# The last pass of a decode backward kernel: a different order of the stages, and buffers kept apart for stores

## The chip, the cores and the metric

The kernel runs on one core of a Trainium2 chip, as one launch. The metric is device time in microseconds. A core has five engines with queues of their own: TensorE (PE, matmuls; PEld is its weight load), VectorE (DVE), ScalarE (ACT), GpSimd (POOL) and SyncE (SP). In this kernel SyncE issues every load from HBM and GpSimd issues every store; the transfers of both run on the core's 16 DMA engines.

## The reference, cut to what matters

One token runs through two layers, twice: attention over a long cache (A), then a two-layer network with a squared ReLU (B), then A and B again with the same weights. The reference gives the output and the gradients of all inputs, the caches among them. The pass that the change touches computes the gradients of the caches and of the queries.

```python
# B, Sq, D = 1, 1, 1024;  Hq, Hkv, Sk, Dh = 32, 4, 65536, 128;  F = 3584
def _A_ref(x, k_cache, v_cache, wq, wo):
    q = (x @ wq).reshape(B, Sq, Hq, Dh).transpose(0, 2, 1, 3)
    k = jnp.repeat(k_cache, rep, axis=1)
    v = jnp.repeat(v_cache, rep, axis=1)
    p = _softmax(jnp.einsum("bhqd,bhkd->bhqk", q, k) * (Dh ** -0.5))
    o = jnp.einsum("bhqk,bhkd->bhqd", p, v)
    return o.transpose(0, 2, 1, 3).reshape(B, Sq, Hq * Dh) @ wo

def _fwd_reference(...):
    x = A_x
    x = x + _A_ref(_layernorm(x), A_k_cache, A_v_cache, A_wq, A_wo)
    x = x + _B_ref(_layernorm(x), B_w1, B_b1, B_w2, B_b2)
    x = x + _A_ref(_layernorm(x), A_k_cache, A_v_cache, A_wq, A_wo)
    x = x + _B_ref(_layernorm(x), B_w1, B_b1, B_w2, B_b2)
    return x
# the result: the output, and jax.vjp of it for grad_out
```

K and V hold 4 groups of 65536 rows of 128 values in bf16, 64 MiB each. Their gradients (out_2 for K, out_3 for V) have the same size. For each cache row and both layers, dP = V dO, dS = P (dP - delta), dV = sum of P dO, dK = sum of dS q, dQ = sum of dS K.

## The kernel before, in words

**Passes.** The kernel reads the caches four times. Passes 1 and 2 are the forward attention of the two layers, pass 3 (`attn_bwd3`) the backward of the second layer's queries, and pass 4 (`attn_bwd4`), the last, does the rest: dQ of the first layer, and dK and dV of both layers together. Between the passes lie dense stages for B and the weights. The change touches pass 4 alone.

**Blocks and items.** A block is 1 MiB of K or V: 32 chunks of 128 rows (`J = 32`). There are 64 blocks of each, 16 per group. Pass 4 goes over 256 items of 8 chunks, four to a block, in a reversed order of groups. For each item, `pipeline` calls a list of stages, each at its own lag in steps:

- `vT` transposes V on TensorE (L1319), and an evacuation (a copy out of PSUM, through `evac`, L161 on ScalarE or L164 on VectorE) writes `kt`. Seven V blocks come out of pass 3 transposed already and skip this.
- `vS` multiplies by dO (L1350) into `ps_sc`; at the end of a block VectorE multiplies by P (L1367) and has dS, called X.
- `eIn` and `eT` copy P of the block on GpSimd (L1328) and transpose it (L1334). P of both layers lies in eight buffers of the arena ("planes", two per group), which are given back when their group is done.
- `dV8` and `dK8` make dV and dK by rank-16 products (`outer16`, L1390): two 512-wide matmuls fill one of two PSUM buffers `ps_gg`, an evacuation writes 1024 columns into a buffer of the arena, and after four of these GpSimd issues a store of 1 MiB (L1396).
- `xT` transposes X for dK; `k8` multiplies K by X into `ps_acc` for dQ (L1421).

**Background work.** `Background.step` is called once per step. It advances the gradients of the weights (`g_outer`, store at L1507; `g_outer_wide`, store at L1528) and the rows of wo and wq that the next group needs (`g_rowdots`: VectorE product at L583, ScalarE sum at L572). The gradient slabs are evacuated through `ps_gg` too (L1467), four evacuations to a 1 MiB store.

**Who sets the order.** Passes 1 to 3 stand in a manual schedule; pass 4 doesn't: a scheduler of the framework orders the instructions of each engine, from the order in which the program emits them and the data they need. Each engine then runs its instructions strictly in that order. So a wait at the head of an engine's queue holds all that is behind it.

**The arena.** Twenty buffers of 1 MiB, of which eight hold P at first. Each load and each store needs one. `take_one` chooses it when the program is built, from a table FREE of when each buffer comes free, counted in steps; a stored buffer counts as free five steps later. Before the change, in pass 4, a load takes the latest freed buffer that has been free for `AHEAD = 9` steps, or else the oldest; an output takes the latest that has been free for one step. Loads and outputs thus take over one another's buffers. A load into a buffer that a store has left waits, on SyncE, until that store has landed.

**Lags before.** `V_SHIFT` lets the V stages lead the others by 16 items (four blocks) at first; the lead falls to nothing over the first 64 items. `eIn` runs 16 steps after its item's number, dV and dK follow at lags 3 and 7 behind it, and `k8` comes last, at lag 11. Two K blocks are loaded before the pass; some loads are issued by hand (`nexts`, with `NOW["newest"]`), and the last three V blocks by `last_v` in one go. dS of the first eight blocks has a buffer of the arena (Xs) until the first group is done; later blocks use three buffers of a pool.

**End.** When dQ of the last group is there, `on4` runs the rows of wq (L667, L699), the layer norm's backward, dx, and the last slab of wq's gradient (`g_outer_last`, L1467, four stores of 512 KiB, L1488).

Of the kernel before, what the change touches and what calls it, by code (L numbers as in the profile page):

```python
# [10 lines left out]
BF = mybir.dt.bfloat16  # L11
# [9 lines left out]
def kernel(  # L21
# [50 lines left out]
    AHEAD = 9  # L72
# [189 lines left out]
    HELD, BUSY = set(), set()  # L262
    NOW = {"step": 0, "pairs": True, "wide": False, "newest": False}
# [19 lines left out]
    def take_one(fill, load=False):  # L283
        by_age = sorted((t, i) for i, t in FREE.items())
        if load and NOW["newest"]:
            i = by_age[-1][1]
            del FREE[i]
            return i
        if load and PS["pass4"]:
            early = [i for t, i in by_age if t <= NOW["step"] - AHEAD]  # L290
            i = early[-1] if early else by_age[0][1]
            del FREE[i]
            return i
        if fill:
# [86 lines left out]
    def touch_order(items, stages):  # L381
        seen, out = set(), []
        at = sorted((k + (lag(k) if callable(lag) else lag), n, k) for n, (t, lag) in enumerate(stages) for k in range(len(items)))
# [13 lines left out]
    B4_LAG = DK_LAG + J // 8  # L397
    DV_LAG = TLEAD + 1
    V_LEAD = 4 * J // 8
    ITEMS = [order_by_unit(False, SU), order_by_unit(True, SU), order_by_unit(False, HB), order_by_unit(True, J)]  # L400
    V_SHIFT = lambda k: min(V_LEAD, max(0, (k - V_LEAD) // 3))
    TOUCH = [touch_order(ITEMS[0], [("k", 0), ("v", FWD_LAG)]), touch_order(ITEMS[1], [("k", 0), ("v", FWD_LAG)]),
             touch_order(ITEMS[2], [("v", 0), ("k", B3_LAG)]), touch_order(ITEMS[3], [("v", V_SHIFT), ("k", B4_LAG + V_LEAD)])]
# [193 lines left out]
    class Rows:  # L597
        def __init__(self, pool=None, bufs=NWT):
            self.pool, self.bufs = pool, bufs
            self.views = deque()  # L600
            self.n = 0
            self.parts = 0
            if pool is None:

                for _ in range(2):
                    t = Slot("s_wt", True).t[:, :].rearrange("p (v a b) -> p v a b", v=4, a=8)
                    self.views.extend(t[:, v, :, :] for v in range(4))
                self.bufs = 8
            self.queue = deque()
            self.jobs = deque()  # L610
            self.feed = None
# [150 lines left out]
    class Background:  # L762
# [35 lines left out]
        def by_group(self, p, gen):  # L798

            order = list(dict.fromkeys(g for g, _ in ITEMS[p]))  # L800
            n = len(ITEMS[p]) // G
            for k, g in enumerate(order[1:]):
                self.later.append((k * n + 8 if PS["pass4"] and k else k * n + n // 4, gen(g), g))
# [21 lines left out]
    def pipeline(items, stages, bg, end=(), holds=(), lead=None):  # L825

        def due(lag):
            at = {}
            for k, it in enumerate(items):
                at.setdefault(k + lag + LEAD if lead is None or lag >= 0 else k + ~lag + lead(k), []).append(it)  # L830
            return at
        LEAD = 0 if lead is None else lead(len(items))
        when = [due(l) for _, l in stages]
        maxlag = max(l for _, l in stages) + LEAD
        for i in range(len(items) + maxlag):
# [11 lines left out]
            bg.step(max(0, i - LEAD))  # L847
# [415 lines left out]
    def attn_bwd4(p, La, Lb, on_group, bg, stack, end=()):  # L1263
# [75 lines left out]
        def vS(g, c8):  # L1339
# [12 lines left out]
            if is_turned("v", g, c8):  # L1352
                kv_done("v", g, c8)
                if c8 % J == J - 8 and nexts:
                    NOW["newest"] = True
                    kv8(*nexts.popleft())
                    NOW["newest"] = False
            if (c8 + 8) % J == 0:
                c0 = c8 + 8 - J
                ps_dp = state["ps_dp"]  # L1360
                if g == items[0][0]:
                    if c8 == J - 8 + items[0][1]:
                        state["Xs"] = Slot("xs", True)
                    X = state["Xs"].t.rearrange("p (n j r) -> p n j r", j=J, r=R2)[:, c0 // J % 8, :, :]
                else:
                    X = dspool.tile([P, J, R2], BF, name="X", tag="X", bufs=3)
# [42 lines left out]
        def k8(g, c8):  # L1409
# [15 lines left out]
            if (g, c8) == items[len(items) // G - 1]:  # L1425
                state["Xs"].free()
# [6 lines left out]
        for b in range(2):  # L1433
            kv8("k", *items[b * J // 8])
        nexts = deque()
        for b in range(V_LEAD * 8 // J // 2):
            nexts.append(("k",) + items[(b + 2) * J // 8])
            nexts.append(("v",) + items[(b + NKEEP[2]) * J // 8])
        pipeline(items, [(vT, ~0), (vS, ~TLEAD), (eIn, 0), (eT, TLEAD), (dV8, DV_LAG), (xT, DK_LAG - 1), (dK8, DK_LAG), (k8, B4_LAG)], bg,
                 end, lead=V_SHIFT)  # L1440

# [28 lines left out]
    def g_outer_last(pool, out_dram, a_cols, b_cols, c0):  # L1470
# [6 lines left out]
        sls = [Slot("og", True) for _ in ras]  # L1477
# [33 lines left out]
    def g_outer_wide(pool, out_dram, nA, nB, a_cols, b_cols):  # L1511

        rsl = Slot("rowbw", True)
# [242 lines left out]
    def last_v():  # L1756

        for g, c8 in ITEMS[3][-3 * J // 8::J // 8]:
            kv8("v", g, c8)

# [8 lines left out]
    attn_bwd4(3, L1, L3, on4, bg, b4, [(12 + B4_LAG, last_v), (20, pre_load("wq4", lambda: wq_slabs(lastg[3], 2))), (10, fill4)])  # L1769
# [32 lines left out]
```

## Time and profile before

| what | value |
|---|---|
| runs of the kernel, median (lowest to highest) | 2014.15 us (2004.31 to 2018.07), 3 runs |
| span of the profiled execution | 2011.2 us; what lies around it isn't listed, the nearest time is the runs' median |
| busy share of the span | PE 81%, PEld 66%, DVE 58%, ACT 52%, POOL 7% |
| DMA over the span | 794.98 MB, mean 395 GB/s; HBM read 624.96 MB, written 165.69 MB |
| pass 4 | about 1215 us to the end |
| loads of pass 4, issue to landing, median | K 11.6 us (61 x 1 MiB), V 11.0 us (57 x 1 MiB) |
| stores of pass 4, issue to landing | 10.4 us median, 21.4 us longest (149 x 1 MiB) |

How to read it: the page's second part cuts the span into 40 slices, with each engine's busy tenths, the clock that TensorE was granted (PEclk) and the DMA's share and rate. A table by stretch gives the same for chosen times: busy us of each engine with its instruction count, then the mean granted clock, the DMA share and GB/s. A row of waits names the waiting engine and line, what it waited for, us in total, times, and the longest. A row of the timeline gives start and duration, engine, line, what is done, and in brackets the idle time before it and what ended it. Times in MB and GB/s are decimal; a buffer of 1 MiB is 1.05 MB.

### The profile page before, as it was taken

Reading aid. Unit: us, or ns where it says so; the run is one execution under the profiler, and the core shown is the slowest. Engines: PE = TensorE matmul, PEld = TensorE weight load, DVE = VectorE, ACT = ScalarE, POOL = GpSimd, SP = SyncE. Lnnn points to the kernel's source line nnn. Section 1 sums busy time; section 2 is a strip of 40 time slices with the busy share of each in tenths; the row PEclk is TensorE's granted clock in tenths of the full one; section 3 lists DMA queues with packets and bytes.
Section 4 is the critical chain, followed back from the end, with each engine's and each line's share of the span. In section 5 each row is a group of like instructions: output and inputs, shape, how many; then the busy total and the mean of one; then the engine's idle time right before and its main releaser. Section 6 shows DMA issues by size and latency. Waiting matters only on the chain. (4 is left out here: it accounts for less than half of the span.)

```text
span 2011.2 us, 67084 instructions
## 1 busy us (share of the span) xinstructions
PE 1627.2 (81%) x30228; PEld 1319.5 (66%) x30228; DVE 1171.7 (58%) x2426; ACT 1045.1 (52%) x1608; POOL 142.9 (7%) x332
## 2 busy tenths in 40 slices
PE   6877788687877777878787888788789799977887
PEld 6877777687777776767777785455455465644554
DVE  5645555255545544435454477656677677866775
ACT  3534344253433453426354365656678576756765
POOL 0000000000000000000000001111111111111211
PEclk9989999699999998899888999878898877888996
DMA  9999999999999998899999987998999999999996
GB/s 390 421 424 420 424 424 402 395 405 420 425 420 424 425 391 335 356 421 424 417 420 412 394 311 284 360 377 350 394 418 424 423 411 370 418 423 388 424 404 243
DMA packets 101037, 794.98 MB, mean 395 GB/s; under 512 B 9472, under 2 KB 9486, under 8 KB 37134
## 3 DMA queue, kind: packets, MB, share of 16 engines
q1 hardware_dynamic: 76670, 624.99, 76.2%
q0 software_dynamic: 24080, 165.70, 20.0%
q8 instruction: 236, 3.87, 0.8%
q14 instruction: 51, 0.42, 0.1%
HBM read 624.96 MB, written 165.69 MB: 393 GB/s over the span
## 5 line engine op out<-in xcount | busy, mean ns | idle before, releaser
L164 DVE COPY kt<-ps_tr 128x1024 bf16<-128x1024 bf16 x724 | 496.4, 688 | 489.8 <-PE ps_tr L1007 252.6
L161 ACT CAST arena<-ps_gg 128x1024 bf16<-128x1024 f32 x457 | 446.9, 1012 | 234.2 <-PE ps_gg L1390 161.6
L1007 PE MATMUL ps_tr<-ident_b,arena 128*128 128x128 bf16 x3840 | 306.9, 224 | 45.6 <-DMA arena<-in_A_k_cache_dram 33.3
L161 ACT COPY kt<-ps_tr 128x1024 bf16<-128x1024 bf16 x164 | 170.9, 1047 | 191.7 <-PE ps_tr L1199 113.5
L1007 PEld LDWEIGHTS <-arena 128*128 128x128 bf16 x3840 | 231.4, 100 | 54.1 <-DMA arena<-in_A_k_cache_dram 36.5
L1109 PE MATMUL ps_acc<-arena 128*128 128x64 bf16 (+4 forms) x4096 | 203.8, 195 | 67.5 <-DMA arena<-in_A_v_cache_dram 53.8
L164 DVE CAST arena<-ps_gg 128x1024 bf16<-128x1024 f32 (+2 forms) x186 | 222.2, 1195 | 61.5 <-PE ps_gg L1390 32.4
L1390 PE MATMUL ps_gg<-GG,xt 64*128 64x512 bf16 x1024 | 221.5, 433 | 21.5 <-ACT arena L161 13.1
L1319 PE MATMUL ps_tr<-ident_b,arena 128*128 128x128 bf16 x1824 | 186.6, 240 | 39.1 <-DMA arena<-in_A_v_cache_dram 37.7
L1109 PEld LDWEIGHTS <-arena 128*128 128x128 bf16 x4096 | 157.7, 100 | 73.2 <-DMA arena<-in_A_v_cache_dram 57.4
L1090 ACT ACTIVATE arena<-S_sb,L_negm 128x128 bf16<-128x128 f32 x256 | 165.5, 1003 | 62.4 <-DVE L_negm L1075 62.4
L1199 PE MATMUL ps_tr<-ident_b,arena 128*128 128x128 bf16 x1920 | 157.9, 229 | 43.8 <-DMA arena<-in_A_v_cache_dram 41.6
L1025 PE MATMUL ps_sc<-L_qpad,kt 128*128 128x64 bf16 (+7 forms) x3584 | 181.7, 193 | 14.2 <-ACT kt L161 6.6
L1319 PEld LDWEIGHTS <-arena 128*128 128x128 bf16 x1824 | 123.9, 107 | 98.0 <-issue 56.1
L1025 PEld LDWEIGHTS <-kt 128*128 128x128 bf16 x3584 | 151.2, 100 | 19.3 <-ACT kt L161 8.9
L1199 PEld LDWEIGHTS <-arena 128*128 128x128 bf16 x1920 | 119.8, 103 | 49.3 <-DMA arena<-in_A_v_cache_dram 44.7
L1421 PEld LDWEIGHTS <-arena 128*128 128x128 bf16 x2048 | 97.8, 105 | 73.4 <-issue 47.5
L1090 ACT ACTIVATION_READ_ACCUMULATOR arena<-S_sb,L_negm 128x1 f32 x256 | 128.1, 500 | 0.0
L1350 PEld LDWEIGHTS <-kt 128*128 128x128 bf16 x1824 | 86.5, 104 | 56.6 <-issue 55.7
L1350 PE MATMUL ps_sc<-DOB,kt 128*128 128x64 bf16 (+3 forms) x1824 | 119.1, 201 | 0.0
L1244 PE MATMUL ps_acc<-dsT,arena 128*128 128x64 bf16 (+7 forms) x2048 | 103.8, 195 | 14.0 <-DMA arena<-in_A_k_cache_dram 10.4
L1421 PE MATMUL ps_acc<-X,arena 128*128 128x64 bf16 (+3 forms) x1536 | 99.6, 203 | 15.7 <-DMA arena<-in_A_k_cache_dram 15.7
(292 smaller groups left out, 2160.7 us busy)
## 6 DMA issues: line engine op xcount, KB each, us to landing
arena<-in_A_k_cache_dram SPq DMA_DIRECT2D x86, 2048.0 KB, 21.3
arena<-in_A_v_cache_dram SPq DMA_DIRECT2D x83, 2048.0 KB, 21.1
out_dram<-arena POOLq DMA_DIRECT2D x149, 1024.0 KB, 10.4
arena<-in_A_v_cache_dram SPq DMA_DIRECT2D x76, 1024.0 KB, 11.7
arena<-in_A_k_cache_dram SPq DMA_DIRECT2D x76, 1024.0 KB, 11.4
arena<-in_B_w_dram SPq DMA_DIRECT2D x32, 896.0 KB, 7.9
arena<-in_A_wo_dram SPq DMA_DIRECT2D x22, 1024.0 KB, 13.6
arena<-in_A_wq_dram SPq DMA_DIRECT2D x20, 1024.0 KB, 14.5
```

What stands on the lines that cost most here:

```text
L161: nc.scalar.copy(out=out, in_=in_)
L164: nc.vector.tensor_copy(out=out, in_=in_)
L1007: nc.tensor.transpose(pt[:, i, :], kb8[:, i, :], ident_b[:, :])
L1025: nc.tensor.matmul(state["ps_s"][:, s:s + w, :].rearrange("p a b -> p (a b)"), lhsT=kt[:, i, :], rhs=L["qpad"][:, g, 0:w, :].rearrange("p ...
L1090: nc.scalar.activation(out=E(p, g, c0, SU)[:, :, h], in_=S[:, h, :], func=ACTF.Exp, bias=L["negm"][:, g, su, h:h + 1], scale=SCALE, accum_ ...
L1109: nc.tensor.matmul(ps_o[:, 0:w, :], lhsT=vb8[:, i, :], rhs=E(p, g, c, w), start=(c % SU == 0), stop=(c % SU == SU - 1), skip_group_check=True)
L1199: nc.tensor.transpose(pt[:, i, :], vb8[:, i, :], ident_b[:, :])
L1244: nc.tensor.matmul(ps_dq[:, 0:w, :].rearrange("p a b -> p (a b)"), lhsT=kb8[:, i, :], rhs=dsT[:, s:s + w, :].rearrange("p a b -> p (a b)") ...
L1319: nc.tensor.transpose(pt[:, i, :], vb8[:, i, :], ident_b[:, :])
L1350: nc.tensor.matmul(state["ps_dp"][:, s:s + w, :].rearrange("p a b -> p (a b)"), lhsT=vt[:, i, :], rhs=DOB[:, g, 0:w, :].rearrange("p a b - ...
L1390: nc.tensor.matmul(pg[:, 512 * h:512 * h + 512], lhsT=xt[64 * h:64 * h + 64, j1 // 8 + m, :], rhs=gg[64 * h:64 * h + 64, :, :].rearrange(" ...
L1421: nc.tensor.matmul(ps_dq[:, 0:w, :].rearrange("p a b -> p (a b)"), lhsT=kb8[:, i, :], rhs=X[:, s:s + w, :].rearrange("p a b -> p (a b)"), ...
```

## The change

The stages of pass 4 get constant lags: `vT` 0, `vS` 2, `k8` 6 (`K4_LAG`), and the output stages `OUT_LAG = 20` steps (five blocks) later than before counted from their item: `eIn` 20, dV at 23, dK at 27. `V_SHIFT`, the lead, `nexts` and `last_v` go. dS of every block goes to the arena buffer Xs, which holds eight blocks and is kept through the whole pass. Three K blocks are loaded before the pass instead of two.

`take_one` keeps up to `NRING = 5` buffers (RING) for outputs, added as they are needed; outputs take the oldest of them, loads and all else take the oldest of the other buffers. After the last `k8` (`NOW["tail"]`) outputs may take any free buffer. The buffers for wt, the last wq slab and the wide rows are no longer counted as outputs. Background work is stepped by the step itself, and the tasks near the end keep their places against the last `k8`. The number of steps, 283, and the bytes moved are the same.

```diff
-    AHEAD = 9
+    NRING = 5
...
     def take_one(fill, load=False):
         by_age = sorted((t, i) for i, t in FREE.items())
-        if load and NOW["newest"]:
-            i = by_age[-1][1]
-            del FREE[i]
-            return i
-        if load and PS["pass4"]:
-            early = [i for t, i in by_age if t <= NOW["step"] - AHEAD]
-            i = early[-1] if early else by_age[0][1]
+        if PS["pass4"]:
+            mine = [i for t, i in by_age if NOW["tail"] or (i in RING) == fill]
+            if fill and len(RING) < NRING and not (mine and FREE[mine[0]] <= NOW["step"]):
+                ready = [i for t, i in by_age if i not in RING and t <= NOW["step"]]
+                if ready:
+                    RING.add(ready[-1])
+                    mine = [ready[-1]]
+            i = mine[0] if mine else by_age[0][1]
             del FREE[i]
             return i
...
-    B4_LAG = DK_LAG + J // 8
+    K4_LAG = TLEAD + J // 8
+    OUT_LAG = 5 * J // 8
...
-                    t = Slot("s_wt", True).t[:, :].rearrange("p (v a b) -> p v a b", v=4, a=8)
+                    t = Slot("s_wt").t[:, :].rearrange("p (v a b) -> p v a b", v=4, a=8)
...
-                self.later.append((k * n + 8 if PS["pass4"] and k else k * n + n // 4, gen(g), g))
+                self.later.append((n // 2 if PS["pass4"] and not k else k * n + (8 if PS["pass4"] else n // 4), gen(g), g))
...
-                if g == items[0][0]:
-                    if c8 == J - 8 + items[0][1]:
-                        state["Xs"] = Slot("xs", True)
-                    X = state["Xs"].t.rearrange("p (n j r) -> p n j r", j=J, r=R2)[:, c0 // J % 8, :, :]
-                else:
-                    X = dspool.tile([P, J, R2], BF, name="X", tag="X", bufs=3)
+                X = Xs.t.rearrange("p (n j r) -> p n j r", j=J, r=R2)[:, c0 // J % 8, :, :]
...
-            if (g, c8) == items[len(items) // G - 1]:
-                state["Xs"].free()
+            if (g, c8) == items[-1]:
+                NOW["tail"] = True
...
-        for b in range(2):
+        Xs = Slot("xs")
+        for b in range(3):
             kv8("k", *items[b * J // 8])
-        nexts = deque()
...
-        pipeline(items, [(vT, ~0), (vS, ~TLEAD), (eIn, 0), (eT, TLEAD), (dV8, DV_LAG), (xT, DK_LAG - 1), (dK8, DK_LAG), (k8, B4_LAG)], bg,
-                 end, lead=V_SHIFT)
+        pipeline(items, [(vT, 0), (vS, TLEAD), (k8, K4_LAG), (eIn, OUT_LAG), (eT, OUT_LAG + TLEAD), (dV8, OUT_LAG + DV_LAG),
+                         (xT, OUT_LAG + DK_LAG - 1), (dK8, OUT_LAG + DK_LAG)], bg, end)
+        Xs.free()
...
-    attn_bwd4(3, L1, L3, on4, bg, b4, [(12 + B4_LAG, last_v), (20, pre_load("wq4", lambda: wq_slabs(lastg[3], 2))), (10, fill4)])
+    attn_bwd4(3, L1, L3, on4, bg, b4, [(20 + OUT_LAG + DK_LAG - K4_LAG, pre_load("wq4", lambda: wq_slabs(lastg[3], 2))),
+                                          (10 + OUT_LAG + DK_LAG - K4_LAG, fill4)])
```

More of the change, by code (lines that the diff above doesn't have):

```diff
@@ L261 @@
     FREE = {i: 0.0 for i in range(NG)}
-    HELD, BUSY = set(), set()
-    NOW = {"step": 0, "pairs": True, "wide": False, "newest": False}
+    HELD, BUSY, RING = set(), set(), set()
+    NOW = {"step": 0, "pairs": True, "wide": False, "tail": False}
     def wide(i):
@@ L382, in touch_order @@
         seen, out = set(), []
-        at = sorted((k + (lag(k) if callable(lag) else lag), n, k) for n, (t, lag) in enumerate(stages) for k in range(len(items)))
+        at = sorted((k + lag, n, k) for n, (t, lag) in enumerate(stages) for k in range(len(items)))
         if True:
@@ L396 @@
     DK_LAG = TLEAD + J // 8 + 1
-    B4_LAG = DK_LAG + J // 8
+    K4_LAG = TLEAD + J // 8
+    OUT_LAG = 5 * J // 8
     DV_LAG = TLEAD + 1
-    V_LEAD = 4 * J // 8
     ITEMS = [order_by_unit(False, SU), order_by_unit(True, SU), order_by_unit(False, HB), order_by_unit(True, J)]
-    V_SHIFT = lambda k: min(V_LEAD, max(0, (k - V_LEAD) // 3))
     TOUCH = [touch_order(ITEMS[0], [("k", 0), ("v", FWD_LAG)]), touch_order(ITEMS[1], [("k", 0), ("v", FWD_LAG)]),
-             touch_order(ITEMS[2], [("v", 0), ("k", B3_LAG)]), touch_order(ITEMS[3], [("v", V_SHIFT), ("k", B4_LAG + V_LEAD)])]
+             touch_order(ITEMS[2], [("v", 0), ("k", B3_LAG)]), touch_order(ITEMS[3], [("v", 0), ("k", K4_LAG)])]
     def plan_keep(p):
@@ L823, in tasks, with pipeline @@
             fn()
-    def pipeline(items, stages, bg, end=(), holds=(), lead=None):
+    def pipeline(items, stages, bg, end=(), holds=()):
         def due(lag):
@@ L829, in due @@
             for k, it in enumerate(items):
-                at.setdefault(k + lag + LEAD if lead is None or lag >= 0 else k + ~lag + lead(k), []).append(it)
+                at.setdefault(k + lag, []).append(it)
             return at
-        LEAD = 0 if lead is None else lead(len(items))
         when = [due(l) for _, l in stages]
-        maxlag = max(l for _, l in stages) + LEAD
+        maxlag = max(l for _, l in stages)
         for i in range(len(items) + maxlag):
@@ L846, in pipeline @@
                     tasks(i)
-            bg.step(max(0, i - LEAD))
+            bg.step(i)
             NOW["wide"] = False
@@ L1353, in vS @@
                 kv_done("v", g, c8)
[L1354 to L1357, printed above, removed]
             if (c8 + 8) % J == 0:
@@ L1432, in attn_bwd4 @@
         start_pass(p)
-        for b in range(2):
+        Xs = Slot("xs")
+        for b in range(3):
             kv8("k", *items[b * J // 8])
-        nexts = deque()
-        for b in range(V_LEAD * 8 // J // 2):
-            nexts.append(("k",) + items[(b + 2) * J // 8])
-            nexts.append(("v",) + items[(b + NKEEP[2]) * J // 8])
-        pipeline(items, [(vT, ~0), (vS, ~TLEAD), (eIn, 0), (eT, TLEAD), (dV8, DV_LAG), (xT, DK_LAG - 1), (dK8, DK_LAG), (k8, B4_LAG)], bg,
-                 end, lead=V_SHIFT)
+        pipeline(items, [(vT, 0), (vS, TLEAD), (k8, K4_LAG), (eIn, OUT_LAG), (eT, OUT_LAG + TLEAD), (dV8, OUT_LAG + DV_LAG),
+                         (xT, OUT_LAG + DK_LAG - 1), (dK8, OUT_LAG + DK_LAG)], bg, end)
+        Xs.free()
     def rows2(cols, halves, rows, f=False):
@@ L1476, in g_outer_last @@
             ras.append(ra)
-        sls = [Slot("og", True) for _ in ras]
+        sls = [Slot("og") for _ in ras]
         yield
@@ L1511, in g_outer_wide @@
     def g_outer_wide(pool, out_dram, nA, nB, a_cols, b_cols):
-        rsl = Slot("rowbw", True)
+        rsl = Slot("rowbw")
         rb = rsl.t
@@ L1754, in on4 @@
             run(PRE["gwq"])
-    def last_v():
-        for g, c8 in ITEMS[3][-3 * J // 8::J // 8]:
-            kv8("v", g, c8)
     def fill4():
```

## The prediction

> **What bounds the kernel now.** I read the page's forty slices first, then the busy table by stretch for the last pass (from 1215 us to the end), then the waits, SyncE's queue and the compute engines apart, then one stall in order of time.
>
> ```profile
> PEclk9989999699999998899888999878898877888996
> DMA  9999999999999998899999987998999999999996
> GB/s 390 421 424 420 424 424 402 395 405 420 425 420 424 425 391 335 356 421 424 417 420 412 394 311 284 360 377 350 394 418 424 423 411 370 418 423 388 424 404 243
> ```
>
> DMA is at nine tenths nearly everywhere; the dips from slice 24 on are the last pass's.
>
> ```profile
> 1215.00:1430.00 215.00, 172.74 (x2071) 105.74 (x2069) 137.67 (x245) 127.43 (x144) 34.67 (x66) 0.81 0.91 354
> 1430.00:1950.00 520.00, 449.56 (x5590) 282.55 (x5588) 369.37 (x655) 361.28 (x430) 91.12 (x171) 0.86 1.00 411
> 1950.00:2012.00 62.00, 48.32 (x557) 29.06 (x555) 38.21 (x76) 36.65 (x39) 10.56 (x17) 0.74 0.67 269
> ```
>
> The last three columns are clock, DMA share, GB/s. The stretches move 76 + 214 + 17 = 307 MB in 797 us. A full slice shows 424 GB/s; at that rate the same bytes take 723 us. So 74 us can be lost or won: 215 x (1 - 354/424) = 35 us at the start, 16 in the middle, 23 at the end. **DMA bounds the pass, and what counts is when it runs dry.**
>
> ```profile
> SPq L350 <- DMA out_dram<-arena: 570.8, 94, 20.1
> SPq L447 <- DMA out_dram<-arena: 82.9, 12, 20.7
> PE ps_tr L1319 <- DMA arena<-in_A_v_cache_dram: 37.7, 12, 8.9
> PE ps_acc L1421 <- DMA arena<-in_A_k_cache_dram: 23.7, 7, 5.8
> ACT arena L161 <- DMA out_dram<-arena: 20.2, 5, 5.2
> DVE arena L164 <- DMA out_dram<-arena: 5.1, 2, 3.8
> ```
>
> SyncE, which issues every load, stands 654 us behind landing stores, because loads take the buffers that stores give back. TensorE then waits 61 us for loads; the evacuations wait only 25 us for buffers. How that empties the DMA:
>
> ```profile
> 1270.29 0.33 SPq L447 DMA_DIRECT2D arena<-in_A_wo_dram  x1
> 1279.18 1.29 DVE L583 TENSOR_TENSOR mv_t<-arena,vbc 128x1024 bf16<-128x1024 bf16 x2 [8.42 <-DMA arena<-in_A_wo_dram]
> 1284.96 0.53 POOL L1396 DMA_DIRECT2D out_dram<-arena  x1 [12.46 <-ACT arena L161]
> ...
> 1260.00:1270.00 10.00, 9.44 (x141) 6.20 (x139) 9.47 (x20) 9.95 (x14) 2.89 (x5) 1.00 1.02 424
> 1270.00:1280.00 10.00, 2.90 (x42) 1.88 (x42) 1.58 (x3) 2.68 (x5) 0.53 (x1) 0.83 1.01 409
> 1290.00:1300.00 10.00, 7.49 (x96) 4.69 (x94) 9.72 (x16) 7.94 (x11) 2.07 (x5) 1.00 0.63 211
> 1300.00:1310.00 10.00, 7.16 (x60) 3.86 (x62) 2.49 (x8) 3.44 (x4) 1.15 (x2) 0.52 1.01 424
> ```
>
> A wo load leaves SyncE late, VectorE stands 8.4 us, no store is issued for 12.5 us, and from 1290 DMA falls to 211 GB/s; then the clock is halved.
>
> **The change, part by part.** The bytes are the same.
>
> *Loads leave the stores' buffers.* In the order of the built programs' instructions, SyncE's waits on store semaphores fall from 138 to 8: every load now follows an engine's last reading. The median distance from release to first use is 347 matmuls for K and 324 for V. Before, it was 367 and 335 for the loads that reused a store's buffer, but counted from the store's issue, and the landing (median 10.4 us) came off it. A full-clock 10 us slice holds about 140 matmuls; the pass's some 8400 in 797 us make 10.5 per us. At that mean pace 340 matmuls are 32 us against a load's landing of 11 us; before, 22 us were left.
>
> *Stores get five buffers.* Evacuation waits on store semaphores on ScalarE and VectorE rise from 112 to 282. The 112 cost 25 us, 0.23 us each, so 282 cost 64 us over two engines with 525 and 545 busy of 797. Behind such a wait stand the V evacuations (kt) and xt, then TensorE. Distance from a store's issue to the next writing of its buffer: median 181 matmuls, 17 us at the mean pace, 13 at full clock; the landing is 10.4 at the median, 21.4 at most. The bounds are nothing and the ring rival below; I take nothing on the end, since a stalled evacuation means stores in flight, and prefetched loads beside them.
>
> *The start.* For 20 steps no dV or dK is made. From 1215 us until the first dV evacuation stand 500 matmuls, 36 us at 14 per us, with 10 loads and 3 gradient stores: 13 MiB, 32 us at 424. About 5 us idle. The rest of the start loses stalls such as that at 1270. Bounds: 0 and the whole 35 saved; I take 22, leaving 13 for these 5, one more stall behind wo or wq (two such loads still have only 120 and 149 matmuls), and the dense stage's wake.
>
> *The middle.* 16 us idle; the three stretches 1650:1700, 1830:1860 and 1860:1950 hold most of it, the first two at 0.94 of DMA. Bounds 0 and 16; I take 10 saved.
>
> *The end gets worse.* The five blocks' lag is never made good. After the last dQ the built program still evacuates and stores 14 buffers of dV and dK and the four half-buffers of the last wq gradient: 64 evacuations through two PSUM buffers. Their price, from the old tail:
>
> ```profile
> 1997.12 1.01 ACT L161 CAST arena<-ps_gg 128x1024 bf16<-128x1024 f32 x1 [2.73 <-PE ps_gg L1467]
> 2003.56 1.01 ACT L161 CAST arena<-ps_gg 128x1024 bf16<-128x1024 f32 x1 [0.71 <-PE ps_gg L1467]
> ```
>
> Between these, both counted, five such run on ScalarE and three on VectorE: 7.45 us for 8, 0.93 each. 64 make 60 us, while 16 MiB need 40: 20 us idle. Add 7 from the last store's issue (2004.86 before, span 2011.2) and 5 before the tail: 32 against 23, so +9. Bounds: -8 (a backlog of stores at the last load covers 15 us) and +17. That the final wq rows and dx now lie beside dV and dK is in this sum.
>
> Removed early loads (last_v, newest) and a third K block up front only move issues: nothing, covered by the seven V blocks already in the arena; without that cover one landing, 11 us. dS kept in the arena for the whole pass costs one buffer; after the first group two planes per group come free.
>
> **Sum:** 2011.2 - 22 - 10 + 9 = 1988 in the profiled execution. Its span lies 3 us under the median of the three runs (2014.15), and what lies around it is not shown; for the median I say 1991.
>
> **Two rules weighed.** 1. The trace's two busy queues together keep 420 to 425 GB/s. The Trainium skill, DMA: Bandwidth & Descriptors, section "Queues, rings and completion order", has each DMA engine take turns between queues packet by packet. Then stores, 166 of the 307 MB, get half while loads wait: 782 us by my estimate, against this change. No row settles it, since before, loads waited for stores. 2. At 1600:1610, 1630:1640 and 1720:1730 the clock stays at 0.50 with TensorE 9.7 to 10.0 us busy. TensorE: Matmul & The Clock Gate, Part 1, restores full clock after some 3.4 us of activity; these rows disagree, so I count a stall's wake at their 73 to 92 matmuls per 10 us.
>
> **Rivals.**
> *Forecast, 0.45:* start and middle won, tail lost: 1966 to 1994.
> *The tail takes it back, 0.28:* the start wins only half (11), the middle 5, the tail costs 17: 2014 - 11 - 5 + 17 = 2015; up to 1995 where only the middle fails. For it: the 0.93 us pace is measured; against: last stores overlap the last loads' backlog.
> *Slower, the ring binds, 0.27:* ScalarE and VectorE stop at the first evacuation into an unlanded buffer, TensorE starves and stays at half clock. A block makes 2.5 stores; a buffer is filled over 7.8 us on average (60 matmuls for dV or dK, some 170 for a gradient slab, at 10.5 per us), then lands. The forecast leaves 797 - 23 - 67 = 707 us for 59 blocks before the tail, 12.0 each; five buffers keep that pace while landing is under 24.0 - 7.8 = 16.2 us, where it decides. At a mean landing of 18 us a block takes 12.9: 0.9 more over 59 blocks is 53, so 2044. For it: median 10.4 now, with loads held back; waits to 20.7. Against: fewer loads in flight when compute stops, so landings shorten.
> That the change doesn't do what it says is excluded by the waits counted.
>
> **Numbers.** Within 1% (about what a measurement of this kernel can tell from no change) is 1994 to 2034. Faster 0.45, same 0.28, slower 0.27. Low end 1966: start saves 30, middle 16, tail costs nothing, 2 more from the landings; high end 2050, past the ring's price.
>
> **What would show it.** Right: SyncE's waits on out_dram nearly gone; 1215:1430 at 390 GB/s or more, the middle at 415 or more; a last stretch of some 60 us without loads at about 270 GB/s; TensorE's waits on V and K under 30 us. Wrong: a mean store landing above 16 us with evacuation waits over 100 us (ring), the middle under 405 GB/s, a clock lower than 0.8, or a tail over 75 us.

## The result, and the profile after

The changed kernel takes **2003.89 us** (median of 20 runs, 1997.52 to 2008.80). The kernel before, measured beside it, takes 2013.83 us (20 runs, 2004.23 to 2020.99). The ratio is 0.9963, with a 95% interval of 0.9949 to 0.9978. By the ratio it is faster by 7.5 us (the medians lie 10 apart), where 23 had been forecast.

The page's slices of the kernel after (TensorE's granted clock, DMA share, GB/s):

```profile
PEclk9999999699999997898888998998998887898885
DMA  9999999999999998999999989999999999999866
GB/s 389 423 423 421 423 425 399 393 394 420 425 420 424 424 404 316 370 422 423 422 415 414 403 309 353 406 423 413 418 398 404 375 425 423 425 422 423 356 259 252
```

The dip at the start of the last pass is smaller: the four slices that had 284, 360, 377 and 350 GB/s now have 353, 406, 423 and 413. The last three slices, 150 us, have fallen to 356, 259 and 252. The table by stretch (us, busy time of each engine, then clock, DMA share, GB/s):

```profile
1215.00:1430.00 215.00, 176.38 (x2481) 114.18 (x2476) 150.76 (x282) 145.26 (x174) 35.72 (x66) 0.91 1.00 407
1430.00:1880.00 450.00, 382.04 (x4886) 240.79 (x4886) 322.61 (x568) 305.29 (x363) 79.81 (x150) 0.87 1.00 413
1880.00:1934.00 54.00, 47.91 (x604) 30.76 (x603) 38.20 (x74) 34.89 (x41) 9.12 (x16) 0.84 0.69 264
1934.00:2002.90 68.90, 44.17 (x241) 14.40 (x237) 37.23 (x53) 39.78 (x42) 12.77 (x22) 0.56 0.63 256
```

Because all versions move the same bytes, the DMA's idle time at 424 GB/s, length x (1 - GB/s / 424), adds up to the differences in time. The same cuts for four kernels, in us; order_alone and ring_alone are the two halves of the change, told of below:

| | before | after | order_alone | ring_alone |
|---|---|---|---|---|
| 1190 to 1215 | 8.3 | 5.9 | 6.0 | 5.4 |
| 1215 to 1430 (start) | 35.5 | 8.6 | 20.3 | 21.3 |
| 1430 to 1880 (middle) | 13.8 | 11.7 | 21.2 | 9.6 |
| 1880 to the end | 23.8 | 47.5 | 40.7 | 21.5 |
| span | 2011.2 | 2002.9 | 2016.8 | 1987.1 |

From before to after the rows add up to -7.7, and the span fell by 8.3. Of the 27 us won at the start, the end takes back 24.

Waits of the kernel after in the last pass (engine, line, what for: us, times, longest):

```profile
SPq L351 <- PE ps_tr L1318: 241.7, 46, 11.9
SPq L351 <- PE ps_acc L1411: 235.3, 40, 30.6
PE ps_gg L1380 <- ACT arena L161: 31.3, 53, 6.3
PE ps_gg L1380 <- DVE arena L164: 27.5, 21, 10.0
PE ps_tr L1318 <- DMA arena<-in_A_v_cache_dram: 2.2, 1, 2.2
ACT arena L161 <- DMA out_dram<-arena: 62.2, 29, 6.3
DVE arena L164 <- DMA out_dram<-arena: 23.0, 10, 4.7
```

SyncE's loads no longer stand behind stores (654 us before) but behind TensorE, which has to be done with a buffer. TensorE waits 2 us for loads (61 before), and the evacuations 85 us for landing stores (25 before). How the end comes about is seen in three views: SyncE's queue (start, us, what it issues), the row of the dQ matmuls (L1411, with first and last start), and the groups of evacuations after 1934 us (times | busy, mean ns | idle before):

```profile
1855.74 0.33 SPq L351 DMA_DIRECT2D arena<-in_A_k_cache_dram  x1
1859.63 0.33 SPq L351 DMA_DIRECT2D arena<-in_A_v_cache_dram  x1
1890.67 8.84 SPq L351 DMA_DIRECT2D arena<-in_A_k_cache_dram  x2
```

```profile
L1411 PE MATMUL ps_acc<-arena x2048: 169/193/261, 1214.9 to 1933.9; 128*128 128x64 bf16 x170, 128*128 128x48 bf16 x6, 128*128 128x32 bf16 x6, 128*128 128x16 bf16 x5
```

```profile
L161 ACT CAST arena<-ps_gg 128x1024 bf16<-128x1024 f32 x39 | 38.6, 1015 | 21.2 <-PE ps_gg L1380 12.5 <-POOL xin L1327 4.6 <-PE ps_gg L1455 3.3
L164 DVE CAST arena<-ps_gg 128x1024 bf16<-128x1024 f32 x24 | 29.4, 1225 | 18.8 <-PE ps_gg L1380 15.1 <-POOL xin L1327 2.2 <-PE ps_gg L1455 1.4
```

After 1860 us only two loads are left. From 1880 to 1934 TensorE is busy for 48 of 54 us, and the DMA has hardly more than the stores that TensorE can produce: 12.0 of the 14.2 MB that it moves. After the last dQ at 1933.9, 63 evacuations of 128x1024 are left, and they take 69 us.

### The profile page after: what moved, and what is told of

It is laid out like the page before. It is cut to its first block, busy times and chain, and to the rows that moved or that the text cites. A ratio compares the mean times of both kernels' runs of the same rounds, so it can differ in the third digit from the quotient of the medians.

```text
span 2002.9 us, 67138 instructions
## 1 busy us (share of the span) xinstructions
PE 1609.4 (80%) x30228; PEld 1303.6 (65%) x30228; DVE 1175.0 (59%) x2424; ACT 1044.0 (52%) x1610; POOL 144.0 (7%) x332
## 5 line engine op out<-in xcount | busy, mean ns | idle before, releaser
L161 ACT CAST arena<-ps_gg 128x1024 bf16<-128x1024 f32 (+1 forms) x457 | 446.0, 1009 | 228.3 <-PE ps_gg L1380 110.5
L1006 PE MATMUL ps_tr<-ident_b,arena 128*128 128x128 bf16 x3840 | 306.2, 224 | 41.4 <-DMA arena<-in_A_k_cache_dram 31.1
L164 DVE CAST arena<-ps_gg 128x1024 bf16<-128x1024 f32 (+1 forms) x186 | 224.2, 1205 | 121.1 <-PE ps_gg L1380 61.7
L1006 PEld LDWEIGHTS <-arena 128*128 128x128 bf16 x3840 | 230.9, 100 | 51.0 <-DMA arena<-in_A_k_cache_dram 33.9
L1108 PEld LDWEIGHTS <-arena 128*128 128x128 bf16 x4096 | 158.1, 100 | 75.1 <-DMA arena<-in_A_v_cache_dram 61.8
L1198 PE MATMUL ps_tr<-ident_b,arena 128*128 128x128 bf16 x1920 | 157.5, 228 | 41.4 <-DMA arena<-in_A_v_cache_dram 37.8
L1318 PE MATMUL ps_tr<-ident_b,arena 128*128 128x128 bf16 x1824 | 174.9, 234 | 4.4 <-DMA arena<-in_A_v_cache_dram 2.2
L1318 PEld LDWEIGHTS <-arena 128*128 128x128 bf16 x1824 | 118.7, 104 | 65.9 <-issue 62.7
L1198 PEld LDWEIGHTS <-arena 128*128 128x128 bf16 x1920 | 119.3, 102 | 46.8 <-DMA arena<-in_A_v_cache_dram 40.3
L1380 PEld LDWEIGHTS <-xt 64*128 64x128 bf16 x1024 | 61.0, 95 | 136.0 <-issue 97.8
L1411 PE MATMUL ps_acc<-arena 128*128 128x64 bf16 (+3 forms) x2048 | 118.9, 199 | 0.4 <-DMA arena<-in_A_k_cache_dram 0.3
L1243 PE MATMUL ps_acc<-dsT,arena 128*128 128x64 bf16 (+7 forms) x2048 | 104.2, 195 | 14.2 <-DMA arena<-in_A_k_cache_dram 10.4
## 6 DMA issues: line engine op xcount, KB each, us to landing
arena<-in_A_k_cache_dram SPq DMA_DIRECT2D x86, 2048.0 KB, 21.3
arena<-in_A_v_cache_dram SPq DMA_DIRECT2D x83, 2048.0 KB, 21.3
out_dram<-arena POOLq DMA_DIRECT2D x149, 1024.0 KB, 13.5
```

The costliest lines, as they stand in the source:

```text
L161: nc.scalar.copy(out=out, in_=in_)
L164: nc.vector.tensor_copy(out=out, in_=in_)
L1006: nc.tensor.transpose(pt[:, i, :], kb8[:, i, :], ident_b[:, :])
L1108: nc.tensor.matmul(ps_o[:, 0:w, :], lhsT=vb8[:, i, :], rhs=E(p, g, c, w), start=(c % SU == 0), stop=(c % SU == SU - 1), skip_group_check=True)
L1198: nc.tensor.transpose(pt[:, i, :], vb8[:, i, :], ident_b[:, :])
L1243: nc.tensor.matmul(ps_dq[:, 0:w, :].rearrange("p a b -> p (a b)"), lhsT=kb8[:, i, :], rhs=dsT[:, s:s + w, :].rearrange("p a b -> p (a b)") ...
```

## The experiments

Times below are medians; each ratio is against the kernel before, run on the same chip. One stage of a single profile is good to some 5 us: the program of ring_alone was profiled twice, at 1987.1 and 1977.4 us, and the medians of its two sets of runs are 1987.95 and 1988.61.

**The two halves of the change.** ring_alone keeps the order of before and takes the buffers of the change; order_alone the reverse.

```diff
 ring_alone: the stages, lags and loads of before, with
-    AHEAD = 9
+    NRING = 5
+ (take_one's branch for the last pass, and the fill flags, as in the change)
 order_alone: the stages and lags of the change, with before's take_one and flags
```

> The old order (V leads by four blocks at first and falls back, outputs close behind at the end) with five buffers for outputs and the others for loads. Theory A: the start is won as in the changed kernel (about 400 GB/s from 1215 to 1430 us) and the end is the old one (about 23 us of idle DMA), so faster than both: 1980 to 1992 us. Theory B (the five store buffers cost): evacuations wait for landing stores for 80 us or more and the time is 2010 us or more.

> The new order of the stages with the old choice of buffers: loads and outputs take over one another's buffers again (129 waits of SyncE on store semaphores, 109 of the evacuations; 8 and 282 in the changed kernel). Theory A (the start is won because loads no longer stand behind landing stores, and the gain is given back in a drain that the five blocks' output lag makes): the start is lost again, 1215 to 1430 us at about 355 GB/s instead of 407, and the drain stays long, so slower than the kernel before, 2020 to 2035 us. Theory B (the order is what won the start, the five store buffers are what costs later): the start stays near 400 GB/s and the time is under the changed kernel's 2004, about 1990.

ring_alone: **1987.95 us, ratio 0.9885 (0.9859 to 0.9912)**, the fastest kernel of this study that does all the work. order_alone: 2015.43 us, 1.0006 (0.9983 to 1.0030). So all of the gain comes from the buffers, and the new order gives 16 us of it back. For ring_alone theory A has the time and the end; the start ran at 382 GB/s, not 400. For order_alone neither theory holds: the start kept 384 GB/s, between the 355 of A and the 400 of B, and the time lies between theirs too. By the table above each half alone wins about 15 us at the start, and the loss at the end comes with the order: 17 us in order_alone, none in ring_alone. ring_alone's table:

```profile
1215.00:1430.00 215.00, 177.17 (x2275) 111.14 (x2275) 149.63 (x276) 137.15 (x158) 37.30 (x71) 0.87 0.96 382
1430.00:1880.00 450.00, 385.84 (x4863) 243.12 (x4861) 328.02 (x574) 320.09 (x386) 80.59 (x153) 0.88 1.00 415
1880.00:1987.10 107.10, 87.91 (x1121) 54.73 (x1119) 72.91 (x140) 68.62 (x74) 18.97 (x31) 0.85 0.85 339
```

Its start is worse than that of the kernel after (382 against 407 GB/s, 13 us) and its end far better (339 against 260 GB/s, 26 us): its last dQ stands at 1967.7, and 13 evacuations are left behind it.

**The lag at the end, and the evacuation of the tail.** lag_shrinks lets the outputs' lag fall from 20 items to 4; tail_split halves each evacuation after the last dQ over both engines.

```diff
 lag_shrinks, in the lags of eIn, eT, dV8, xT, dK8:
-OUT_LAG
+OUT_LAG - min(16, max(0, (k - 64) // 8))          # k: the item's number
 tail_split, in outer16 (o is the part of stg that evac wrote):
-                evac(stg[...], pg[:, :], kind="f32")
+                if NOW["tail"]:
+                    nc.scalar.copy(out=o[:, 0:512], in_=pg[:, 0:512])
+                    nc.vector.tensor_copy(out=o[:, 512:1024], in_=pg[:, 512:1024])
...
+                else:
+                    evac(o, pg[:, :], kind="f32")
```

> The changed kernel, but the outputs' lag shrinks from 20 items to 4 between item 64 and item 192, so that the last dV and dK follow the last V and K closely. Theory A (the drain is made by the output lag): the last stretch without loads falls from about 100 us to about 60, idle DMA there from 45 us to about 25, time 1980 to 1990 us. Rival C (the drain is made by loads that run ahead, since they have all other buffers, and by TensorE and the evacuations behind them): loads end at the same place, the idle time stays within 10 us of the changed kernel's, time 1998 to 2008 us.

> The changed kernel, but after the last dQ each 1024-wide evacuation of dV and dK is cut in two halves, one on ScalarE (0.58 us for 512 columns) and one on VectorE (0.69 us), at the same time. Theory A (the tail is paced by the two PSUM buffers' round trip, 0.93 us an evacuation): 56 of them at about 0.7 us save 12 us, time 1990 to 1994 us. Rival D (the tail is paced by TensorE at half clock or by the stores): within 3 us of 2004.

lag_shrinks: 2001.49 us, 0.9960 (0.9936 to 0.9983). Its tail is 32 us shorter (37 us with 32 evacuations), but the last dQ came 30 us later, with 24.4 us of idle DMA in the middle. The time is rival C's, but the loads did not end at the same place, and the end idled 34.5 us, between the kernel after (47.5) and theory A (25). tail_split: 2007.29 us, 0.9983 (0.9959 to 1.0007), no gain. It doesn't tell what it was made for, since the two halves ran one after the other:

```profile
1960.41 0.59 ACT L1386 CAST arena<-ps_gg 128x512 bf16<-128x512 f32 x1 [0.18 <-issue]
...
1961.03 0.69 DVE L1387 CAST arena<-ps_gg 128x512 bf16<-128x512 f32 x1 [0.56 <-ACT arena L1386]
```

Together they take 1.31 us, no less than a whole evacuation (1.0 us on ScalarE, 1.2 on VectorE).

**A lag of two blocks, and earlier row loads.**

```diff
 lag_two:
-    OUT_LAG = 5 * J // 8
+    OUT_LAG = 2 * J // 8
 after_rows_early, and the same three edits on ring_alone in ring_rows_early:
-        steps = 8 if PS["pass4"] else WAIT_STEPS
+        steps = 12 if PS["pass4"] else WAIT_STEPS
 and wo's and wq's slabs loaded with ahead=2 in the last pass, not 1
```

> The new kernel with its outputs (dV and dK) two blocks behind in place of five (8 items, not 20); everything else as it is, the five store buffers too. In the profile of the new kernel the last pass leaves 8.6 us of DMA idle in 1215 to 1430 us, 11.7 in 1430 to 1880 and 47.5 from 1880 to the end (at 424 GB/s a full slice). Theory E (the lag buys the start and is paid back at the end, buffer for buffer: about five and a half stores fewer are left behind the last dQ, some 24 evacuations of 0.93 us, 22 us): the end falls to 30 or less, the start rises to 12 to 18, sum some 58: 1990 to 1997. Theory F (the middle gives back whatever the end saves, as with the shrinking lag): 1999 to 2004. Theory G (the order dQ right behind V is what costs, the lag nothing): 2000 to 2008, with the end above 40.

> The new kernel with the row loads (wo and wq) issued one slab earlier in the last pass and their products four steps later. It prices the middle: in the new kernel VectorE stood 6.6 and 9.8 us behind two wq loads and DMA fell to 319 to 384 GB/s between 1540 and 1590 us. Theory H (those stalls hold the compute back, and what compute lacks in the middle is the end's price): VectorE's waits on wq and wo fall under 3 us, TensorE's wait at L1346 for VectorE (13 us) goes, and the time falls by 8 to 14: 1989 to 1996. Rival: the row loads take two more buffers from V and K and the lead shrinks, or the stores' five buffers are what holds compute back (its evacuations wait 85 us): no change, 1999 to 2006.

> ring_alone (order of before, five store buffers) with the row loads one slab earlier and their products four steps later. In ring_alone one wq load leaves VectorE standing 11.8 us at 1690 to 1702 us, TensorE 8.5 us behind it, and DMA falls to 230 GB/s at 1700 to 1710. Theory H: that stall goes and the time falls by 5 to 9 us: 1978 to 1983. Rival (the early slabs take buffers that V and K lack, whose waits grow): 1987 to 1996.

lag_two: 2012.63 us, 1.0029 (1.0012 to 1.0046), slower than five blocks and than all three theories had it. The end idled 42.8 us, above 40, as only G had said. after_rows_early: 2000.20 us, 0.9968 (0.9943 to 0.9993), which can't be told from the kernel after: VectorE's waits for wq and wo are gone, as theory H had it, but the time is its rival's. ring_rows_early: 1994.63 us, 0.9930 (0.9911 to 0.9949), in the rival's range and rather worse than ring_alone, though the intervals touch: TensorE's wait for VectorE at L1368 fell from 8.5 us to 3.4, but evacuations waited 83 us for stores in place of 66, and the start idled 27 us. What lag_two lost shows in VectorE's waits: 21.2 us behind wq in two waits, the longer of them 15.1:

```profile
DVE mv_t L583 <- DMA arena<-in_A_wq_dram: 21.2, 2, 15.1
```

**Both together, and one block.** lag_two_rows_early and lag_one_rows_early take the early row loads with a lag of two blocks and of one; shrink_rows_early takes them with the shrinking lag.

> The new kernel with the lag of two blocks and the row loads early. With the lag of two blocks alone VectorE stood 27 us behind two wq loads (15.1 at most) and TensorE 22 behind VectorE; last dQ came at 1968.5 us, no earlier than with the order of before, and the tail after it was 44 us against 69 with five blocks. Theory R (a stall behind row loads is what the shorter lag lost, the tail's 0.99 us per evacuation is the order's price): those waits go, last dQ at 1945 to 1955, time 1988 to 1998. Theory S (the shorter lag loses its work elsewhere, in evacuations that wait for stores, or in the loads): 2004 to 2013, rows or not.

> The new kernel with the outputs one block behind (4 items) and the row loads early. With early rows, five blocks gave 2000.2 us and two gave 1991.0 (start 11.7 and 16.2 us of idle DMA, last dQ at 1931.6 and 1955.5, tails of 61 and 35 us). Theory R (the lag buys idle at the start and is paid back in the tail at 0.99 us per evacuation): start 17 to 22, tail some 30, time 1985 to 1993. Theory T (below two blocks the start loses as much as the tail saves, as TensorE then waits for K and V, 32 us at two blocks): 1994 to 2004.

> The new kernel with the output lag that shrinks from 20 items to 4 between items 64 and 192, as in lag_shrinks (2001.5 us: start 9.1 us of idle DMA, middle 24.4, tail 37), and the row loads early. Theory R (only the stalls behind wq, 18 us of VectorE there, kept the shrinking lag from its gain): middle falls to 8 to 14, time 1982 to 1991, the least of all orders. Theory U (the extra outputs between items 64 and 192 wait for landing stores, 94 us of evacuation waits there against 85 in the new kernel, and that is what the middle lost): middle stays above 18, time 1994 to 2002.

lag_two_rows_early: **1991.02 us, 0.9905 (0.9874 to 0.9937)**: theory R holds, the wait at L583 is gone, and with early rows two blocks beat five by 9 us. That is level with ring_alone within the intervals. lag_one_rows_early: 1999.35 us, 0.9951 (0.9929 to 0.9973), theory T, though its price did not come from K and V (30 us of TensorE's waits, 32 at two blocks): the middle idled 17.0 us. shrink_rows_early: 2001.21 us, 0.9958 (0.9938 to 0.9977), theory U by its time, with 24.4 us idle in the middle. So a shorter lag shortens the tail, as the table below shows, and below two blocks the middle loses more than that.

**Is it the DMA or the compute that sets the end?** Here half of every K and V load of the last pass is left out, and the compute goes over what stood in the buffers; all else is as it was.

```diff
+                hw = J // 2 if PS["pass4"] else J
-                nc.sync.dma_start(out=sl.t.rearrange("p (j d) -> p j d", d=DH), in_=half(KVIN[t], g, hb))
+                nc.sync.dma_start(out=sl.t.rearrange("p (j d) -> p j d", d=DH)[:, 0:hw, :], in_=half(KVIN[t], g, hb)[:, 0:hw, :])
```

> The new kernel with half of every K and V load of the last pass left out (the first 16 of a block's 32 columns are loaded, the other half of the buffer keeps what stood there), all compute, stores, buffers and waits as they are. It prices the compute chain by itself. The loads of K and V are about 127 MB, so some 63 MB go, 150 us at 424 GB/s. Theory D (the DMA's bytes set the pass, idle stays as it is): 1845 to 1880. Theory K (from 1430 us on, TensorE with its evacuations and their store waits sets the end, and the loads only run ahead of it): 1950 to 1995, with the DMA far from full in the middle, TensorE idle as much as in the new kernel, and the last dQ still some 69 us ahead of the end.

> ring_alone (order of before, five store buffers) with the same half of every K and V load of the last pass left out. Theory D: 1830 to 1865, as far below ring_alone's 1988 as the other is below the new kernel. Theory K: 1935 to 1975, and below the new kernel's half-load time by about the 16 us that stand between the two with full loads. If this one falls much further than the other, the order of before was held by its loads and the new order by its compute.

after_half_loads: 1893.57 us, 0.9423 (0.9384 to 0.9463); ring_half_loads: 1884.93, 0.9380 (0.9337 to 0.9423). Neither theory holds whole. The table of after_half_loads, cut at its last dQ:

```profile
1215.00:1430.00 215.00, 195.20 (x2814) 127.81 (x2812) 171.21 (x311) 162.79 (x195) 40.13 (x75) 0.95 0.94 365
1430.00:1823.00 393.00, 364.21 (x5169) 236.09 (x5167) 339.82 (x616) 320.23 (x383) 86.03 (x159) 1.00 0.96 375
1823.00:1891.90 68.90, 43.86 (x246) 14.54 (x242) 37.24 (x54) 39.99 (x42) 12.79 (x22) 0.58 0.64 256
```

The last dQ came at 1823.0 in place of 1933.9, 111 of the 150 us that the bytes would give, with TensorE then busy for 364 of 393 us. **The tail stayed at 69 us.** So the loads' bytes hold what stands ahead of the last dQ, until TensorE is busy for 93% of it. ring_half_loads shows the same: 107 us before its last dQ, and a tail of 19.6 us (19.4 with all loads).

In the tail no load of K or V is left to be halved, so this run doesn't tell what paces it. The trace of the kernel after does in part: from 1936 us on no evacuation waits for a store, and the stores land soon after their issue (the row gives their number, the KB of each and the median us to landing; over the whole pass that is 13.5):

```profile
out_dram<-arena POOLq DMA_DIRECT2D x14, 1024.0 KB, 4.2
```

So there the DMA waits for the evacuations, and not they for it.

**The price of the tail.** From the last dQ matmul to the end, and the 128x1024 evacuations in it:

| | evacuations | us |
|---|---|---|
| ring_alone | 13 | 19.4 |
| before | 14 | 23.5 |
| shrink_rows_early | 21 | 28.5 |
| lag_one_rows_early | 21 | 30.0 |
| lag_two_rows_early | 29 | 35.3 |
| lag_shrinks | 32 | 37.3 |
| lag_two | 39 | 44.1 |
| order_alone | 53 | 58.3 |
| after_rows_early | 53 | 61.1 |
| after | 63 | 69.0 |

From 13 to 63 it is (69.0 - 19.4) / 50 = 0.99 us for each. An evacuation fills 256 KiB of a store, which the DMA moves in 0.62 us at 424 GB/s. Whatever is left behind the last load thus costs 0.37 us more than its bytes.

tail_three gave the tail a third pair of PSUM banks.

```diff
+                if NOW["tail"] and state["nth"] % 3 == 0:
+                    for h, pg in enumerate((ps_sc([P, 512]), ps_tr([P, 512], F32))):
+                        ... the same matmul into pg, and an evacuation of 128x512 ...
+                    continue
                 pg = ps_gg()
```

> The new kernel with a third pair of PSUM banks for dV and dK after the last dQ (every third 128x1024 result goes to two single banks, which nothing else needs by then, and leaves as two 128x512 evacuations). In the profiles so far the time from the last dQ matmul to the end is 19.4 us with 13 such evacuations left, 37 with 32, 44 with 39, 61 with 53, 69 with 63: 0.99 us each. Theory P (two PSUM buffers pace the tail: each waits for its matmuls, its evacuation and two semaphores): 0.75 each, the tail 52 to 58 in place of 69, the time 1988 to 1995. Theory Q (TensorE at half clock or the stores' landing pace it): the tail stays at 65 or more, 1999 to 2007.

1999.97 us, 0.9955 (0.9935 to 0.9974): theory Q by the tail, which took 65.9 us for 51 whole and 26 half evacuations. A third pair of PSUM buffers thus takes 3 us off the tail, and not 11 to 17; by the landings above the stores don't pace it either. The granted clock in it is 0.57, with TensorE busy two thirds of the time; whether the clock is cause or effect wasn't tried.

**Do five store buffers hold the compute back?** This was my rival for a slower kernel.

```diff
 ring_seven (on ring_alone), after_ring_seven (on the new kernel), shrink_rows_seven:
-    NRING = 5
+    NRING = 7
 after_seven_used and ring_seven_used also:
-            if fill and len(RING) < NRING and not (mine and FREE[mine[0]] <= NOW["step"]):
+            if fill and len(RING) < NRING:
```

> The order of before with store buffers of their own as in ring_alone (1988 us), but seven in place of five. With five, evacuations stand 66 us behind store landings (ScalarE 43.9, VectorE 22.2) and TensorE loses about 27 us in the waits for L1470's PSUM buffers and 22 for L1391's. Theory A (five is a shade too few): the evacuation waits fall under 35 us and the time to 1978 to 1986. Rival (the two buffers are missed by the loads, whose waits for K and V grow from 27 us): 1990 to 2000, idle at the start above 25 us. Neither matters: 1985 to 1991.

> The new kernel with seven store buffers in place of five. With five its evacuations stand 85 us behind store landings (ScalarE 62.2, VectorE 23.0) and TensorE 59 behind evacuations at the outer products. Theory U (that ring holds the compute back, and so the end): evacuation waits under 55 us, last dQ at 1920 to 1928 in place of 1933.9, tail still 69, time 1990 to 1997. Rival (as with the order of before, where seven gave 1988.6 and five 1988.0 us: landings stretch with the number in flight, and the loads lack two buffers): 1999 to 2008.

> The shrinking lag with early row loads (2001.2 us; start 20.3 us of idle DMA, middle 24.4, from 1880 on 24.8) and seven store buffers in place of five. Theory U (its extra outputs between items 64 and 192 wait for landing stores, 83 us in all, and the middle's idle is theirs): evacuation waits under 55 us, middle under 16, time 1988 to 1995. Rival: the loads lack the two buffers, start above 22 us, time 1999 to 2008.

The first two changed nothing, and for a plain reason: the choice takes a further buffer only when the oldest isn't due by the planned steps, and it never took a sixth. ring_seven is ring_alone instruction for instruction (1988.61 us, 0.9897, 0.9860 to 0.9933); after_ring_seven differs from the kernel after in the last one per cent of TensorE's instructions (2003.66 us, 0.9963, 0.9948 to 0.9978). They serve as repeats. shrink_rows_seven did become another program (1998.01 us, 0.9938, 0.9915 to 0.9961, against 0.9958 without); its middle idled 12.7 us, its waits for stores fell from 83 us to 65, and the two intervals overlap.

> The new kernel with seven store buffers that are all used: the count was raised to seven before, but a further buffer was taken only where the oldest was not yet due by the planned steps, and the built program kept to five (its instructions differ from the new kernel's in the last one per cent alone). Here the count is filled at once, and each of seven buffers carries some 20 stores in place of 28. Theory U (five buffers hold the compute back): evacuation waits under 45 us in place of 85 to 89, last dQ at 1915 to 1928 in place of 1934 to 1942, time 1988 to 1997. Rival (the two buffers are missed by the loads, and landings grow with the stores in flight): TensorE's waits for K and V above 15 us, time 1999 to 2010.

> The order of before with seven store buffers that are all used (ring_alone and the run with the count of seven are one program with five, 1988.0 and 1988.6 us). Theory U: evacuation waits under 35 us in place of 60 to 66, time 1978 to 1985. Rival (loads lack the two): TensorE's waits for K and V above 35 us in place of 24 to 27, time 1990 to 2002.

after_seven_used: **2016.63 us, 1.0033 (1.0014 to 1.0052)**, 13 us slower than with five. Its rows of waits:

```profile
ACT arena L161 <- DMA out_dram<-arena: 2.9, 1, 2.9
DVE arena L164 <- DMA out_dram<-arena: 2.4, 2, 2.2
PE ps_acc L1411 <- DMA arena<-in_A_k_cache_dram: 30.5, 10, 6.1
PE ps_tr L1318 <- DMA arena<-in_A_v_cache_dram: 20.2, 13, 3.9
```

and its start in the table by stretch:

```profile
1215.00:1430.00 215.00, 176.88 (x2276) 112.18 (x2274) 139.61 (x251) 133.88 (x160) 31.82 (x60) 0.84 0.96 373
```

The evacuations' waits are gone, 5 us in place of 85, and nothing is won. TensorE now waits 51 us for K and V, and the start idles 26 us in place of 9. ring_seven_used: 1991.27 us, 0.9914 (0.9882 to 0.9947), no better than with five; VectorE there stands 62 us behind wo and wq loads (12 in ring_alone). So the 85 us cost less than two of the loads' buffers would; what they cost by themselves these runs don't show. Landings did not stretch (11.2 us at the median, 13.5 with five).

## Why the prediction was right or wrong

**The sum.** The forecast was -22 at the start, -10 in the middle, +9 at the end: -23. Measured were -27, -2 and +24, and -2 ahead of the pass: -8. The sign and the first term were right, the other two were mis-sized: the end by 15 us, the middle by 8.

**"Loads leave the stores' buffers", "The start": right.** SyncE's waits on stores are gone, the start runs at 407 GB/s, TensorE waits 2 us for loads. The gain was 27 where I took 22.

**"Stores get five buffers": low in its size, and its price open.** 85 us of waits where 64 were estimated. Seven buffers in use took them away and made the kernel slower, and the median landing rose from 10.4 to 13.5 us, under the 16.2 where the ring would have decided: the rival "the ring binds", at 2044, is out. That the waits cost nothing, as I took it, is not shown. At least once in the middle one kept TensorE:

```profile
1544.74 1.93 ACT L161 CAST arena<-ps_gg 128x1024 bf16<-128x1024 f32 x2 [3.90 <-DMA out_dram<-arena]
1545.80 0.61 PE L1455 MATMUL ps_gg<-rowb,rowa 2*128 2x512 bf16 x2 [3.71 <-ACT arena L161]
```

**"The middle": mis-sized, 2 us saved and not 10.** It ran at 413 GB/s, where 415 was to show it. The stalls at 1650 and 1830 went, and new ones came at 1540 to 1590 (319 to 384 GB/s): the one just shown, and at 1574 VectorE standing 6.6 us behind a wq load. I had named such a stall once, for the start, where it came too (9.8 us behind wq, to 1392); the row loads were not moved by the change, and the prediction had counted their slack but not carried it into the middle. With the rows loaded early the middle ran at 416 GB/s, but the time can't be told from that of the kernel after.

**"The end gets worse": the step that failed, by the term "5 before the tail".** The tail itself was right: 63 evacuations for 64, 0.99 us each for 0.93, 69 us for 60 + 7, and 27 us idle in it, as 20 + 7 had said (the 7 is 6.3 by the two times given for it). But from 1880 to 1934 the DMA idled 54 x (1 - 264 / 424) = 20 us, not 5. Three more profiles with the same order and buffers up to the last dQ (after_ring_seven, tail_split, tail_three) have 19 to 22 there. The loads are through by 1860 but for two blocks, and the compute is not: the DMA is left with the stores of a TensorE that is busy for 48 of the 54 us. I bounded this loss by -8 and +17, for which no sum stands (32 less the 15 covered, against 23, is -6), and took a small value.

What brings it is the order. order_alone, where loads still stand 577 us behind stores, idles 18 us between 1880 and its last dQ and 23 behind it. ring_alone, where they don't, idles 12 and 9, as the kernel before does (12 and 12). The new order issues its last K or V load some 100 us ahead of the end (at 1899 of 2003 us, in order_alone at 1899 of 2017). The old order has loads to the last: in ring_alone SyncE still issues four K loads from 1886.75 to 1932, 55 us ahead of the end. Loads that run ahead because they no longer wait for stores may add to it, since the end of the kernel after idles 7 us more than that of order_alone, but no run shows that.

**The rivals.** "The tail takes it back" was the nearest by its number: it gave 2015, or 1995 where only the middle fails; the start won in full and both middle and end failed, at 2004. That the time lies between its two values is in part luck: it put the loss into the tail, which cost what the forecast had said, and the loss stood ahead of the tail.

**The rules weighed.** The turns between queues stay unsettled. From 1430 to 1880 us the stores' queue moved 94.9 MB and the loads' queue 90.4, about half each, but before the change, with loads that waited for stores, it was 94.0 and 90.0: the halves may be what the kernel needs. The 782 us of that estimate lie near the measured 788, but of the 65 us above 723 some 48 stand after 1880 us, where hardly a load is left. As for the clock, from 1890 to 1900 us it stays at 0.50 with TensorE busy all 10 us, as in the rows of before.

**What stays open.** Why the tail takes 0.99 us for an evacuation; and why, with early rows, one block and the shrinking lag lose 17 and 24 us in the middle, where two blocks lost 10.6.

## What to carry to other kernels

When a kernel is bound by transfers, add up the idle time of the DMA by stretch, and ask which work an order leaves behind the last loads: price it by its own pace (here 0.99 us for 256 KiB) against the pace of its bytes (0.62), and price the stretch ahead of it too, in which the loads have run out and the compute has not (20 us here). Taking loads and stores out of each other's buffers was worth 21 to 23 us by itself; the new order of the stages cost 16 of them. Before an experiment on a count, look whether the built program uses it.

## What the runs showed of the hardware

- In the tail, where stores run alone, a 1 MiB store landed 4.2 us after its issue at the median, no evacuation waited for one, and the rate was 256 GB/s: that of the producer, not of the DMA.
- With two buffers moved from the loads to the stores, the evacuations' waits for stores fell from 85 us to 5, TensorE's waits for loads of K and V rose from 2 us to 51, and the time rose by 13 us.
- In the tail of the kernel after, the granted clock was 0.56 over 69 us with TensorE busy for 44 of them.
- One and the same program gave spans 10 us apart (1987.1 and 1977.4 us), of which 6 us arose ahead of the last pass's first dQ matmul: it started at 1221.4 us in the one and at 1215.3 in the other.
